# A fused attention and Fourier-mixing kernel on one core: the first batch's softmax sums leave TensorE, and the weights' rounding is spread into the second batch

## The chip, the cores and the metric

One core of a Trainium2 chip runs the whole kernel. The engines are named as in the profile: PE (TensorE matmuls), PEld (its weight loads), DVE (VectorE), ACT (ScalarE), POOL (GpSimd), SP (SyncE, which issues most DMAs). The metric is the device time of one execution in microseconds (us); less is better.

## The reference, cut to what matters

Four batches of eight heads over 768 positions with 64 columns each. Block-sparse attention, then a Fourier mixing block with a feed-forward part over 512 columns:

```python
scores = scale * np.matmul(q, k.transpose(0, 1, 3, 2))
scores = np.where(mask, scores, -1000000000.0)
scores = scores - np.max(scores, axis=-1, keepdims=True)
attn = np.exp(scores)
attn = attn / (np.sum(attn, axis=-1, keepdims=True) + 1e-09)
x = ...  # matmul(attn, v), heads side by side: (4, 768, 512)
mixed = np.real(np.fft.fft(np.fft.fft(x, axis=1), axis=2))
u = x + mixed
un = (u - mean(u)) / np.sqrt(var(u) + 1e-06)
out = u + np.maximum(un @ w_ch1, 0.0) @ w_ch2   # 512 x 2048, 2048 x 512
```

The mask is made from 32 x 32 blocks, some of them drawn at random. The two weights arrive in float64.

## The kernel before

**Attention in slots.** Heads are taken in 16 pairs, four to a batch. A pair has 12 units (two halves of the queries, six chunks of 128 keys), and a *slot* is two units, so a pair has six slots, a batch 24, the whole attention 96. `slot(sl)` writes the instructions of one slot: `scores` (the products `s`, L573, and for the first batches the mask as a second product, L583), `weigh` (the exponential on ScalarE, L593, into one of four `e` buffers), and, for the slot before, `values` (products `o` with v, L647). At the end of a pair the results are turned and copied into `x` (`place`). For pairs 5 and on, q and k are transposed by VectorE (`flip_blocks`, L540) and q put in order by ScalarE (`in_order`, L548).

**The softmax sums.** The sum over keys of every query is needed to divide by. Batch 0 gets it on TensorE: `add_up` multiplies each `e` by a column of ones into the PSUM tile `sp` (L714), and `into_sums` adds it to `sums`. In batches 1 to 3 `gather` adds the six chunks of a half into `acc`, either in one addition on VectorE (L628) or in two of half the width on GpSimd (L633), whichever the planner thinks sooner (the last two units of a pair always on GpSimd); `total` then needs only one set of products a pair (L728). An `e` buffer is free when both its values and its addition are done.

**The mixing.** When a batch's attention is complete, `begin(b)` queues its mixing in `apart`, a list in fixed order: `norm_steps` (`invert` turns the sums and takes reciprocals, `scale_x` multiplies, L756), eight folds on VectorE (`fold_0`, ...; L779 to L807), four products along the sequence (`along`, `zp`), three across (`across`, `pq`), then for each of six tiles `arrive`, `spread` (statistics), `whiten`, `un_flip` (transposes `utp`, copies) and the sums `left` and `right` for a Strassen product. At its end `go()` moves the channel steps into `late`: eight `quad` (seven products each, L1045) and 24 `channels` (L1101); it also ends the masking by products. While batch b mixes, batch b+1's attention goes on.

**The planner.** The order on each engine is written by the program itself (`manual_schedule`), by a ledger `when` of planned times: `busy(engine, us)` adds a price, and `gap` takes the next step of `apart` only if the ledger says that its inputs are ready and that VectorE isn't more than a few us ahead (`AHEAD`, `ALONE`). `until(met)` takes steps whether or not they are ready, until a condition holds. One of these is hard: `x` has two buffers, so in slot 53 the first result of batch 2 has to wait `until(lambda: (b - 2, 0) in finished)`, that is until all channel steps of batch 0's first half are written.

**The weights.** They come as 32 chunks of 128 x 512, which a DMA brings raw (float64) into one of five rooms (`W_ROOMS` 0, 1, 3, 4, 5 of the pool `big`; the mixing uses the same rooms later), and `w_round` rounds to float32: two ScalarE operations (L460, L463) and five on VectorE (L464 to L472), priced 1.2 and 3.0. `w_loads` and `w_steps` stand at the end of each slot; with `W_PACE = 1.42` chunks a slot, all 32 are rounded by slot 22, all of `w_ch1` first.

Of the kernel before, what the change touches and what calls it, by code (L numbers as in the profile page):

```python
# [102 lines left out]
def kernel(  # L103
# [332 lines left out]
    WN = 512  # L436
    wchunks = []
    for w, w_sb in ((w_ch1, w1_sb), (w_ch2, w2_sb)):
        rows, cols = w.shape
        words = _words(w, rows * cols)  # L440
        for row in range(rows // P):
            for col in range(0, cols, WN):
                src = bass.AP(tensor=words, offset=2 * (row * P * cols + col),
                              ap=[[2 * cols, P], [1, 2 * WN]])
                wchunks.append((src, w_sb[:, row, col:col + WN]))
    wraw = {}
    W_ROOMS = (0, 1, 3, 4, 5)

    def w_load(i):
        t = room(W_ROOMS[i % len(W_ROOMS)], [P, 3 * WN], "wraw", U32)  # L450
        nc.sync.dma_start(out=t[:, 0:2 * WN].bitcast(I32), in_=wchunks[i][0])
        wraw[i] = t

    def w_round(i):
        t = wraw.pop(i)
        dst = wchunks[i][1]
        pair = t[:, 0:2 * WN].rearrange("p (n two) -> p n two", two=2)
        lo, hi, a = pair[:, :, 0], pair[:, :, 1], t[:, 2 * WN:3 * WN]

        nc.scalar.mul(out=lo.bitcast(FP32), in_=lo, mul=2.0 ** -52)  # L460


        nc.scalar.mul(out=a.bitcast(FP32), in_=hi.bitcast(FP32), mul=2.0 ** -112)  # L463
        nc.vector.tensor_scalar(out=a, in0=a, scalar1=3, scalar2=0x7FFFFFFF,  # L464
                                op0=ALU.logical_shift_left, op1=ALU.bitwise_and)
        nc.vector.scalar_tensor_tensor(out=dst.bitcast(U32), in0=hi, scalar=0x80000000, in1=a,
                                       op0=ALU.bitwise_and, op1=ALU.bitwise_or)

        nc.vector.tensor_scalar(out=a, in0=dst.bitcast(U32), scalar1=0xFF800000, scalar2=None,
                                op0=ALU.bitwise_and)  # L470
        nc.vector.tensor_mul(out=a.bitcast(FP32), in0=lo.bitcast(FP32), in1=a.bitcast(FP32))
        nc.vector.tensor_add(out=dst, in0=dst, in1=a.bitcast(FP32))  # L472
        busy("DVE", 3.0, busy("ACT", 1.2))
# [11 lines left out]
    turned, e_of, acc_of, o_of, sums_of, x_of, sp_of = {}, {}, {}, {}, {}, {}, {}  # L485
# [101 lines left out]
    def weigh(u, s):  # L587
        n, w = divmod(u, UP)
        half, c = divmod(w, C)
        e = ep.tile([P, 2, HS], FP32, tag="e", name="e")  # L590
        e_of[u] = e
        if u in by_pe:
            nc.scalar.activation(out=e, in_=s[:, :, 0:HS], func=ACT.Exp, scale=scale)  # L593
            e_at[u] = busy("ACT", 0.8, max(s_at[u], e_free.pop(u - 2 * SLOT, 0.0))) + HOP
            if n >= NP:
                to_gather.append(u)

            if w >= UP - SLOT:
                gather_to(u)
        else:  # L600
            nc.scalar.activation(out=s[:, :, 0:HS], in_=s[:, :, 0:HS], func=ACT.Exp, scale=scale)  # L601
            m = mask[:, c, half * HS:(half + 1) * HS].rearrange("p (o s) -> p o s", o=1)
            nc.vector.tensor_tensor(out=e, in0=s[:, :, 0:HS], in1=m.broadcast_to([P, 2, HS]),  # L603
                                    op=ALU.mult)
            e_at[u] = busy("DVE", 0.97, busy("ACT", 0.8, s_at[u]) + HOP) + HOP
            gather_to(u)
            if n >= NP:
                gather(u)
# [5 lines left out]
    def gather(u):  # L614
# [11 lines left out]
        sooner = max(when["DVE"], at) + 1.0 < max(when["POOL"], at) + 2.9  # L626
# [3 lines left out]
        else:  # L630
# [3 lines left out]
            acc_at[n, half] = busy("POOL", 2.9, at) + HOP  # L634
# [55 lines left out]
    def into_sums(key, j, sp):  # L690
        if j == 0:
            if key == (0, 1):
                sums_of[key] = un_p.tile([P, DM], FP32, tag="un", name="sums")[:, 0:HS]
            else:
                sums_of[key] = sum_p.tile([P, HS], FP32, tag="sums", name="sums")
# [3 lines left out]

    def add_up(us):  # L700


        n, w = divmod(us[0], UP)
        half, c = divmod(w, C)
        j = pairs[n][1]
        if c == 0:
            sp_of[n, half] = ps_m.tile([P, 512], FP32, tag="m", name="sp"), bank("m")
        sp, at = sp_of[n, half]
        sp = sp[:, 0:HS]
        busy("PE", 0.85)  # L710
        for r, u in enumerate(us):
            for i in range(2):
                g = BLK * (2 * i + r)
                nc.tensor.matmul(sp[g:g + BLK, :], pick[:, BLK - j:2 * BLK - j], e_of[u][:, i, :],  # L714
                                 start=(c == 0), stop=(c == C - SLOT), tile_position=(0, g))
        if c == C - SLOT:
            into_sums((0, half), j, sp)
            give(at, busy("DVE", 0.6, when["PE"] + HOP))
# [14 lines left out]
    def norm_steps(b):  # L733
# [3 lines left out]
        def invert(half):  # L737
            sums = sums_of.pop((0, half) if b == 0 else b)
# [4 lines left out]
            if b > 0:  # L743
                nc.vector.reciprocal(out=r, in_=st[:, :, :, 0:NP])
                return
            for i in range(2):
                to = r[:, :, 2 * half + i, :]
                nc.vector.tensor_copy(out=to, in_=st[:, :, 2 * i, 0:NP])
                nc.vector.tensor_tensor(out=to, in0=st[:, :, 2 * i + 1, 0:NP], in1=to, op=ALU.add)
            if half == 1:  # L750
                nc.vector.reciprocal(out=r, in_=r)
# [7 lines left out]
        return ([("t", lambda h=h: invert(h), 0.45, 0.0, 0.9) for h in range(2 if b == 0 else 1)] +  # L759
# [8 lines left out]
    def fourier(b, xA, xB, uns):  # L768
# [6 lines left out]
        def fold_0(i):  # L775
            if i == 0:
                st["f"] = (room(0, [P, T, DM], "sa"), room(1, [P, T, DM], "sd"),
                           un_p.tile([P, DM], FP32, tag="un", name="e1"))
# [114 lines left out]
        def arrive(half, m):  # L893
# [13 lines left out]
            tt(out=ends, in0=un[:, 0:M + 1:M], in1=ends, op=ALU.add)  # L907

# [47 lines left out]
    def mixer(b, xA, xB):  # L956
# [27 lines left out]
        def spare_room():  # L984
            if s:
                return
            rest, n, w = room(5, [P, ND * HS], "t4"), HS * ND // 2, P * ND // 2
# [25 lines left out]
        def left(p, j):  # L1013
# [3 lines left out]
            spare_room()  # L1017
            a11, a12, s2, a22 = blocks(p)
# [78 lines left out]
        def channels(r, half, m):  # L1097

            y, at = ps_m.tile([P, DM], FP32, tag="m", name="y"), bank("m")
# [150 lines left out]
    W_PACE = 1.42  # L1250
# [3 lines left out]
    state = {"paired": False, "total": None, "w": 0, "got": 0, "owed": 0.0, "ready": 0.0}  # L1254
# [91 lines left out]
    def w_loads():  # L1346
        while state["got"] < min(len(wchunks), state["w"] + len(W_ROOMS)):
            w_load(state["got"])
            state["got"] += 1

    def w_steps(sl):
        while state["w"] < min(len(wchunks), W_PACE * sl):
            w_round(state["w"])
            state["w"] += 1

    def slot(sl):
# [7 lines left out]
        def sum_up():  # L1364
# [5 lines left out]
            if at < SB:  # L1370
                add_up(done)
# [57 lines left out]
        if sl > SB and s == 0 and sl <= B * SB:  # L1429
# [66 lines left out]
    w_load(0)  # L1496
    load_q(1)
    w_load(1)
    load_k(1)
    state["got"] = 2  # L1500
# [118 lines left out]
```

## Time and profile before

| what | us |
|---|---|
| median of 3 runs | 1062.0 (1061.76 to 1062.73) |
| span of the profiled execution | 1059.7 |
| PE busy | 1036.7 |
| DVE busy | 654.7 |
| ACT busy | 374.3 |
| POOL busy | 235.6 |
| `add_up` products (L714) | 20.5 busy |
| `total` products (L728) | 10.9 busy |

The profiled execution is a run of its own; the page gives its span, from the first instruction to the last, and that span is what the trace's durations are added up against. It is 2.3 us shorter than the median of the timed runs. A matmul in float32 shows as two instructions (x192 for 96 products). In a timeline the columns are start, length, engine, line, operation, output and inputs, count, and in brackets the idle time before and what ended it. In a table of groups the numbers behind the bar are busy us, mean ns of one, and the idle time before them.

### The profile page before, as it was taken

Reading aid. Unit: us, or ns where it says so; the run is one execution under the profiler, and the core shown is the slowest. Engines: PE = TensorE matmul, PEld = TensorE weight load, DVE = VectorE, ACT = ScalarE, POOL = GpSimd, SP = SyncE. Lnnn points to the kernel's source line nnn. Section 1 sums busy time; section 2 is a strip of 40 time slices with the busy share of each in tenths; the row PEclk is TensorE's granted clock in tenths of the full one; section 3 lists DMA queues with packets and bytes.
Section 4 is the critical chain, followed back from the end, with each engine's and each line's share of the span. In section 5 each row is a group of like instructions: output and inputs, shape, how many; then the busy total and the mean of one; then the engine's idle time right before and its main releaser. Section 6 shows DMA issues by size and latency. Waiting matters only on the chain.

```text
span 1059.7 us, 12422 instructions
## 1 busy us (share of the span) xinstructions
PE 1036.7 (98%) x4390; PEld 535.8 (51%) x4390; DVE 654.7 (62%) x1218; ACT 374.3 (35%) x742; POOL 235.6 (22%) x262
## 2 busy tenths in 40 slices
PE   8999999999999999999999999999999999999996
PEld 4333345444455554444444555444445554578575
DVE  6898894667645445664668364765457455575663
ACT  6978855664030112342441302253220211210210
POOL 1000183537000002454553001256520001000000
PEclk9999999999999999999999999999999999999998
DMA  7757422220000002212220001221000001000001
GB/s 214 231 168 232 117 46 45 45 47 15 1 0 1 1 0 48 59 29 54 42 54 2 1 0 30 60 38 28 11 11 6 1 0 32 29 0 1 1 20 43
DMA packets 120803, 46.65 MB, mean 44 GB/s; under 512 B 108176, under 2 KB 113822, under 8 KB 120734
## 3 DMA queue, kind: packets, MB, share of 16 engines
q1 hardware_dynamic: 119484, 45.06, 17.3%
q10 hardware_dynamic: 1218, 0.72, 0.3%
q8 instruction: 36, 0.59, 0.2%
q14 instruction: 33, 0.27, 0.1%
q0 software_dynamic: 32, 0.01, 0.0%
HBM read 37.11 MB, written 6.29 MB: 41 GB/s over the span
## 4 chain that ended last, share of the span: by engine, by line
PE 89%; DVE 4%; DMA 3%; ACT 2%; issue 1%; SPq 0%; POOL 0%; ACTq 0%; DVEq 0%
PE y L1101 23%; PE z L1045 15%; PE s L573 12%; PE o L647 10%; PE yp L1045 7%; PE yy L1164 7%; PE xp L1045 4%; PE zp L855 2%; DMA out_dram<-x 1%; PE s L583 1%; PE zp L827 1%; PE sp L714 1%; PE sp L728 1%; PE utp L970 1%; PE xt L670 1%
## 5 line engine op out<-in xcount | busy, mean ns | idle before, releaser
L633 POOL TENSOR_TENSOR acc<-acc,e 128x384 f32<-128x384 f32 x158 | 159.3, 1042 | 94.1 <-DVE e L603 75.1
L573 PE MATMUL s<-qT,kT 64*128 64x384 f32 x768 | 154.0, 516 | 7.7 <-ACT e L593 4.3
L647 PE MATMUL o<-e,vr 128*64 128x384 f32 x768 | 141.8, 497 | 0.0
L1101 PE MATMUL y<-w_sb,hB 128*128 128x512 f32 x288 | 128.2, 596 | 1.0 <-DVE x L1104 1.0
L1101 PE MATMUL y<-w_sb,hA 128*128 128x512 f32 x288 | 128.4, 595 | 0.0
L603 DVE TENSOR_TENSOR e<-s,mask 128x768 f32<-128x768 f32 x92 | 83.8, 951 | 57.6 <-ACT s L601 47.8
L1104 DVE TENSOR_TENSOR x<-y,x 128x512 f32<-128x512 f32 x72 | 49.7, 690 | 110.9 <-PE y L1101 110.8
L573 PEld LDWEIGHTS s<-qT,kT 64*128 64x128 f32 x768 | 64.2, 186 | 85.8 <-issue 22.1
L601 ACT ACTIVATE s<-s 128x768 f32<-128x768 f32 x92 | 69.9, 792 | 87.5 <-PE s L573 87.0
L1045 PE MATMUL z<-unT,t 128*128 128x384 f32 x256 | 93.1, 486 | 1.2 <-DVE hA L1050 1.2
L633 POOL TENSOR_TENSOR acc<-e 128x384 f32<-128x384 f32 x42 | 47.1, 1142 | 211.6 <-ACT e L593 126.7
L1050 DVE TENSOR_TENSOR hA<-z,hA 128x384 f32<-128x384 f32 x64 | 35.7, 557 | 87.5 <-PE z L1045 87.5
L593 ACT ACTIVATE e<-s 128x768 f32<-128x768 f32 x100 | 76.1, 815 | 36.2 <-PE s L583 31.2
L1101 PEld LDWEIGHTS y<-w_sb,hB 128*128 128x128 f32 x288 | 53.4, 190 | 67.7 <-issue 65.0
L918 POOL TENSOR_SCALAR st<-st 128x1 f32<-128x1 f32 x24 | 8.6, 358 | 346.9 <-DVE st L917 346.8
L1101 PEld LDWEIGHTS y<-w_sb,hA 128*128 128x128 f32 x288 | 53.3, 190 | 62.8 <-issue 59.7
L647 PEld LDWEIGHTS o<-e,vr 128*64 128x64 f32 x768 | 47.9, 136 | 70.3 <-issue 67.9
L1054 ACT ACTIVATE hA<-hA 128x384 f32<-128x384 f32 x64 | 33.5, 523 | 120.3 <-DVE hA L1050 119.9
L1045 PEld LDWEIGHTS z<-unT,t 128*128 128x128 f32 x256 | 48.5, 190 | 35.5 <-DVE hA L1050 2.1
L1054 ACT ACTIVATE hB<-hB 128x384 f32<-128x384 f32 x64 | 33.5, 523 | 86.5 <-DVE hB L1050 84.2
L1065 ACT COPY hA<-xp 128x384 f32<-128x384 f32 x32 | 15.3, 478 | 97.9 <-PE xp L1045 97.9
L1045 PE MATMUL xp<-unT,w_sb 128*128 128x384 f32 x128 | 47.2, 492 | 0.0
(202 smaller groups left out, 1428.7 us busy)
## 6 DMA issues: line engine op xcount, KB each, us to landing
wraw<-in_moe_w_ch_dram SPq DMA_DIRECT2D x32, 512.0 KB
vr<-in_v_dram SPq DMA_DIRECT2D x30, 192.0 KB
qb<-in_q_dram SPq DMA_DIRECT2D x44, 96.0 KB
kb<-in_k_dram SPq DMA_DIRECT2D x44, 96.0 KB
x<-oT SPq DMA_DIRECT2D x192, 12.0 KB
out_dram<-x SPq DMA_DIRECT2D x15, 128.0 KB
out_dram<-x SPq DMA_DIRECT2D x7, 256.0 KB
qr<-in_q_dram SPq DMA_DIRECT2D x24, 64.0 KB
```

Source lines behind the costliest of these rows:

```text
L573: nc.tensor.matmul(s[:, i, 0:HS], kT[rows, c * P:(c + 1) * P], qT[rows, queries], start=True, stop=u not in by_pe)
L593: nc.scalar.activation(out=e, in_=s[:, :, 0:HS], func=ACT.Exp, scale=scale)
L601: nc.scalar.activation(out=s[:, :, 0:HS], in_=s[:, :, 0:HS], func=ACT.Exp, scale=scale)
L603: nc.vector.tensor_tensor(out=e, in0=s[:, :, 0:HS], in1=m.broadcast_to([P, 2, HS]), op=ALU.mult)
L633: nc.gpsimd.tensor_add(out=acc[:, i, :], in0=start[:, i, :], in1=e[:, i, :])
L647: nc.tensor.matmul(o[D * i:D * i + D, :], vt[:, i, c, :], e[:, i, :], start=(c == 0), stop=(c == C - 1))
L1045: nc.tensor.matmul(to, a[:, k, :], c[:, k, :], start=(k == 0), stop=(k == ND // 2 - 1))
L1050: tt(out=to, in0=ps, in1=a, op=ALU.add)
L1054: nc.scalar.activation(out=h, in_=h, func=ACT.Relu)
L1101: nc.tensor.matmul(y, hs[0, half][:, l, m * P:(m + 1) * P], w2_sb[:, 4 * r + l, :], start=(l == 0), stop=(l == 3))
L1104: nc.vector.tensor_tensor(out=x[:, m, :], in0=y, in1=x[:, m, :], op=ALU.add)
L1164: nc.tensor.matmul(ps, a[:, k, :], c[k // 2][:, k % 2, :] if isinstance(c, list) else c[:, k, :], start=(k == 0), stop=(k == 3))
```

## The change

Four things, in one diff. (1) Batch 0's sums go the way of the other batches: `add_up` and the second `invert` are gone, `gather` runs for all batches, `total` for all pairs. (2) The chunks are listed in the order in which the channel steps need them: four of `w_ch1`, four of `w_ch2`, and so on. (3) `W_PACE` is 0.6: `w_until(int(0.6 * sl))` at the end of each slot, so that 14 chunks are rounded by slot 24 and the last ones in slots 52 to 54; `w_until` in `left`, `spare_room` and `channels` rounds at once what a step needs. (4) A raw chunk takes any room that is free; `w_leave` gives rooms back to the mixing, rounding first what lies in them: 0 and 1 at `fold_0` (returned after the last `arrive` of batch 0), 3, 4 and 5 at `spare_room`. The planner's prices for a rounding (3.0 to 3.6 on VectorE) and for an addition on GpSimd (2.9 to 2.2) change too.

```diff
+    for r in range(NF // 4):
+        wchunks += [wchunk(w_ch1, w1_sb, row, r * WN) for row in range(ND)]
+        wchunks += [wchunk(w_ch2, w2_sb, 4 * r + l, 0) for l in range(4)]
+    wraw, w_room = {}, {}
+    w_state = {"got": 0, "done": 0, "rooms": (0, 1, 3, 4, 5)}
+
+    def w_load():
+        i = w_state["got"]
+        if i == len(wchunks):
+            return False
+        free_of = [r for r in w_state["rooms"] if r not in w_room.values()]
+        if not free_of:
+            return False
+        w_room[i] = free_of[0]
+        t = room(w_room[i], [P, 3 * WN], "wraw", U32)
         nc.sync.dma_start(out=t[:, 0:2 * WN].bitcast(I32), in_=wchunks[i][0])
         wraw[i] = t
+        w_state["got"] += 1
+        return True
+
+    def w_until(n):
+        while w_state["done"] < min(n, len(wchunks)):
+            if w_state["done"] == w_state["got"]:
+                w_load()
+            w_round(w_state["done"])
+            del w_room[w_state["done"]]
+            w_state["done"] += 1
+
+    def w_leave(*rooms, to=None):
+        if w_state["done"] < len(wchunks):
+            w_state["rooms"] = tuple(r for r in w_state["rooms"] if r not in rooms)
+            w_until(max([i + 1 for i, r in w_room.items() if r in rooms], default=0))
+            w_state["rooms"] += tuple(to or ())
...
-        busy("DVE", 3.0, busy("ACT", 1.2))
+        busy("DVE", 3.6, busy("ACT", 1.2))
...
-            if n >= NP:
-                to_gather.append(u)
+            to_gather.append(u)
...
-        sooner = max(when["DVE"], at) + 1.0 < max(when["POOL"], at) + 2.9
+        sooner = max(when["DVE"], at) + 1.0 < max(when["POOL"], at) + 2.2
...
-    def add_up(us):
...
         def fold_0(i):
             if i == 0:
+                w_leave(0, 1)
...
+            if m == 1 and half == 1 and b == 0:
+                w_leave(to=(0, 1))
...
         def spare_room():
             if s:
                 return
+            w_leave(3, 4, 5)
+            w_until(8)
...
+            w_until(8 * (p // 2) + 4)
...
+            w_until(8 * r + 8)
...
-    W_PACE = 1.42
+    W_PACE = 0.6
...
     def w_steps(sl):
-        while state["w"] < min(len(wchunks), W_PACE * sl):
-            w_round(state["w"])
-            state["w"] += 1
+        w_until(int(W_PACE * sl))
...
-            if at < SB:
-                add_up(done)
...
-        if sl > SB and s == 0 and sl <= B * SB:
+        if 0 < sl <= B * SB and s == 0:
             short.append(("t", acc_at[n - 1, 1], lambda: total(n - 1)))
```

## The prediction

> **What bounds the kernel now.** I read the shares by slice first, then the chain that ended last, then stages. The chain is TensorE's almost everywhere:
>
> ```profile
> PE   8999999999999999999999999999999999999996
> DVE  6898894667645445664668364765457455575663
> POOL 1000183537000002454553001256520001000000
> ...
> PE 89%; DVE 4%; DMA 3%; ACT 2%; issue 1%; SPq 0%; POOL 0%; ACTq 0%; DVEq 0%
> ```
>
> So a microsecond taken from TensorE's queue is worth a microsecond, as long as no other engine becomes late. The two stages that the change touches are the first batch (slots 2 to 23, 15.84 to 123.33 us) and the second up to its first channel product (123.33 to 241.80). The stage table (length, then busy time of PE, PEld, DVE, ACT, POOL):
>
> ```profile
> 15.84:123.33 107.49, 103.36 (x694) 41.58 (x693) 95.21 (x204) 93.11 (x193) 0.00 (x0) 0.98 0.67 201
> 123.33:241.80 118.47, 117.50 (x717) 54.10 (x717) 82.92 (x134) 73.85 (x146) 61.10 (x58) 1.00 0.25 48
> 161.00:178.00 17.00, 17.00 (x87) 8.93 (x85) 6.37 (x6) 9.27 (x21) 5.92 (x6) 1.00 0.19 31
> ```
>
> In both TensorE is the bound, but VectorE has only 12 us to spare in the first and 35.6 in the second, of which 10.6 lie in 161 to 178, where the mixing waits for TensorE's `zp` products. GpSimd is idle in the first.
>
> **First batch, TensorE.** The groups by form, the one long stall in TensorE's timeline, and its cause among the waits (us in total, times, longest):
>
> ```profile
> L714 PE MATMUL sp<-e,pick 128*32 128x384 f32 x192 | 20.5, 498 | 0.0
> L728 PE MATMUL sp<-acc,pick 128*32 128x384 f32 x96 | 10.9, 497 | 0.1
> ...
> 66.76 0.85 PE L714 MATMUL sp<-e,pick 128*32 128x384 f32 x8
> 70.01 2.46 PE L573 MATMUL s<-qT,kT 64*128 64x384 f32 x8 [2.40 <-ACT e L593]
> ...
> 76.11 1.56 PE L573 MATMUL s<-qT,kT 64*128 64x384 f32 x8
> ...
> ACT wraw L460 <- DMA wraw<-in_moe_w_ch_dram: 3.8, 2, 3.3
> ```
>
> `add_up` runs once in each of 24 slots. Start to next start it takes 0.78 us (14.25 to 15.03): 24 x 0.78 = 18.7 us removed. `total`, 0.79 us (182.00 to 182.79), is added for four pairs, three of them inside the stage: +2.4, the fourth +0.8 after it; one of two sums transposes (133.94 to 134.42) goes, -0.5. At 67.6 ScalarE waits 3.3 us for a raw chunk and TensorE stands for 2.40; then the matmuls up to the next scores take 6.2 us (70.01 to 76.19) for work that takes 4.6 elsewhere. Rounding 0.6 chunks a slot instead of 1.42 asks for about 19 chunks in this stage (14 rounded, 5 raw) instead of 32, so I take these 2.4 + 1.6 = 4.0 us as gone too.
>
> A slot then needs 4.89 - 0.78 - 0.18 + 0.11 = 4.04 us of TensorE (4.89 is 107.49 / 22). Can the others keep that pace? VectorE: a chunk takes 2.97 us (18.75 to 21.73), so 1.8 a slot, and tables and sums 0.4. The sums are ten additions a pair, 1.67 a slot, at 1.04 us on VectorE (L628) or about 2.2 on GpSimd (two of 1.04 to 1.14, L633). One on GpSimd and 0.67 on VectorE gives GpSimd 2.2 and VectorE 2.9 of 4.04. ScalarE loses 18 chunks x 1.14 us. So they fit, but the two disturb each other:
>
> ```profile
> 124.78 0.69 DVE L472 TENSOR_TENSOR w_sb<-w_sb,wraw 128x512 f32<-128x512 f32 x1
> ...
> 126.56 0.43 DVE L469 TENSOR_SCALAR wraw<-w_sb 128x512 uint32<-128x512 uint32 x1
> 127.03 1.37 DVE L471 TENSOR_TENSOR wraw<-wraw 128x512 f32<-128x512 f32 x1
> 128.43 1.37 DVE L472 TENSOR_TENSOR w_sb<-w_sb,wraw 128x512 f32<-128x512 f32 x1
> ...
> 126.75 2.50 POOL L633 TENSOR_TENSOR acc<-e 128x384 f32<-128x384 f32 x2 [121.65 <-ACT e L593]
> ```
>
> The moment GpSimd adds, the two-tensor operations of the rounding double: a chunk beside GpSimd takes 2.97 + 2 x 0.68 = 4.33 us. With GpSimd busy for half a slot that is 0.4 us more a slot on VectorE, 3.3 in all: still inside 4.04. For late additions that hold an `e` buffer I put 2.5 us (between 0 and 8). The second batch therefore starts 18.7 - 2.4 + 4.0 - 2.5 = 17.8 us earlier; with the fourth total and the transpose, 17.5.
>
> **Second batch: what the rounding meets there.** Until now it was free of rounding but for a tail of 6.1 us (the L464 to L472 rows up to 129.73). By the pace, 14 chunks are done by slot 24 and 31 by slot 52, whatever else waits: 17 chunks, 17 x 2.97 = 50.5 us on VectorE alone, 73.6 beside GpSimd. VectorE's sum: 82.9 - 6.1 + 50.5 = 127.3 us if its own additions (20.5 us, L628) stay. If they all go to GpSimd, that has 61.1 + 20 x 2.2 = 105 of 118 us, is beside the rounding nearly always, and VectorE has 76.8 - 20.5 + 73.6 = 129.9. Either way some 128 us, against this much of TensorE before the channel products must start:
>
> ```profile
> 241.82 1.46 PE L1045 MATMUL xp<-unT,w_sb 128*128 128x384 f32 x4
> ...
> 256.74 1.72 PE L573 MATMUL s<-qT,kT 64*128 64x384 f32 x8
> 258.39 1.56 PE L1045 MATMUL xp<-unT,w_sb 128*128 128x384 f32 x4
> ...
> 409.07 1.56 PE L573 MATMUL s<-qT,kT 64*128 64x384 f32 x8
> ```
>
> The last scores before a long stretch of products stand at 256.74: slot 53, after which the third batch needs the tiles that batch 0 holds, and the program lets no attention through until batch 0 is finished. The mixing now reaches its first product at 241.82 with 6.0 us of attention left (252.37 to 258.39). So TensorE has 118.5 + 6.0 = 124.5 us of other work for the second batch's VectorE chain to hide under, and 1.7 more when the mask products of slots 50 to 53 (0.42 each) come back, since `go()` comes later.
>
> Add to 128 the idle time that the chain's own dependences force: 35.6 today; rounding fills part of it; 10 to 15 stay, the 161 to 178 kind. That is 138 to 143 us, TensorE idle for 12 to 17 at the wall. The second way to the same number goes by order. The rounding at each slot's end isn't asked whether there is room, while a mixing step is placed only if VectorE's planned lead stays under 3 to 4.5 us. At the planner's price of 3.6 us each and 3 chunks in 5 slots, mixing gets only the rest; walking down the slots by those prices, I have `fold_0` in slot 34 instead of 28, with three chunks at once in front of it (`w_leave(0, 1)`), and at slot 53 everything from the second `spread` on still to do. At the trace's durations these steps are: five `spread` 3.9, five `whiten` 2.3, one `across` 0.8, two `arrive` 1.7, `left` with one chunk 4.1, `right` 4.3: 17 us of VectorE, and 7 of product, transpose, copy and GpSimd waits between them, with 5.5 us of TensorE in it: 18.5 idle. I take 19 (between 4 and 28), since there nothing covers it. Two queues stand behind a backlog on VectorE: ScalarE's `in_order` copies wait for VectorE's transpose of q and hold the exponentials behind them; SP's weight loads wait for a room and hold the q, k, v loads. Both have a slot or more of slack, so I cost them at nothing; without it, each is a slot's 3 to 4 us.
>
> After the gap the matmuls start slow, as at 70.01: +1.6. The Trainium skill ("TensorE: Matmul & The Clock Gate", Part 1) has the clock fall only after an idle window of about 3.4 us; 2.40 us sufficed in the rows above, so the rows decide, and by the page this term would be nought.
>
> **Sum** against the profiled execution, 1059.7 us: -17.5 + 19 + 1.6 + 1.7 = +4.8, 1064.5. The median of the runs shown is 1062.0, 2.3 above the span: 1066.8, say 1066. What follows the wall has no part in the change: one chunk is left, under products. Under 0.2% (2.1 us) a measurement of this kernel can't tell from no change.
>
> **The rivals.**
> - *The second batch absorbs the rounding* (faster). The chain is ahead of my ledger because rounding falls into the 161 to 178 kind of hole and the real chunk is 2.97, not 3.6. It decides the sign where the idle time at the wall is under 14 us. With 6 us left: 1062 - 17.5 + 6 + 1.7 = 1052; with none 1046. For it: VectorE's idle 35.6 us; against: 128 of 124.5. Chance 0.33.
> - *GpSimd and VectorE bind the first batch too* (slower still). If all five operations of a chunk double beside GpSimd, a chunk is 5.9 us, 3.6 a slot, and with 1.1 of other work VectorE passes 4.04: the slot grows to 4.6, 12 us of the 17.5 are lost, and the wall is no earlier: 1062 - 5.5 + 22.3 = 1079. The L469 row (0.43 with GpSimd beside it for its second half) speaks against. The Trainium skill ("GPSIMD Engine Reference", Key points) speaks for it: contention with every VectorE instruction that has two SBUF inputs or a two-port mode. Chance 0.12.
> - *The pace is not what sets the rounding*: rooms that leave force the chunks at two points, and in between nothing is rounded, the chain runs free and the wall idles some 14: about 1062, no change. Chance 0.08.
>
> **How the numbers follow.** The forecast has 0.47, its own range 1058 to 1073 (idle 11 to 26). Its low edge lends 0.04 to faster and 0.03 to same. Faster: 0.33 + 0.04 = 0.37. Same: 0.08 + 0.03 = 0.11. Slower: 0.40 + 0.12 = 0.52. The range of 8 in 10 leaves out half of the second rival and the best end of the first: 1048 to 1077.
>
> **What would show it.** Right: no L714; slot 24 some 18 us earlier; scores of slot 23 about 4.1 us apart; VectorE over 95% busy from there to the wall; `fold_0` five or more slots later; before the first `xp` a stretch of 15 to 25 us in which TensorE does transposes and stands. Wrong: the first `xp` still two slots before the last scores, or first-batch slots over 4.5 us.

## The result, and the profile after

The kernel after takes 1100.95 us (1099.45 to 1101.06), the kernel before on the same chip 1062.03: a ratio of 1.0364 (1.0349 to 1.0378). Forecast were 1066 us and a range of 1048 to 1077, so the sign was right and the size was not. The profiled execution spans 1099.3 us, 39.6 more than before. The page of after, its slices and its chain:

```profile
PE   8998966988699999999999999999999999999996
DVE  5887988899874544565567646575456455575663
POOL 4877874766400000154547000155450001000000
PEclk9999986999799999999999999999999999999999
...
PE 78%; DVE 13%; issue 3%; ACT 2%; DMA 2%; SPq 1%; POOL 0%; DVEq 0%; ACTq 0%
```

Nearly all that changed lies in the first 11 slices. There GpSimd is busy for 4 to 8 tenths of every slice, TensorE shows a 6 in slices 6, 7 and 11, the clock falls to 6 and 7 tenths in the last two of these, and VectorE's share of the chain goes from 4% to 13%. The stages, in the columns of the stage table of before (length; busy PE, PEld, DVE, ACT, POOL; clock). The first two rows are slots 2 to 23 and slot 24 to the first channel product; that second stretch is called *the stage* from here on. The third row is its worst stretch, the fourth is from slot 53 to that product:

```profile
15.02:113.01 97.99, 91.64 (x543) 39.55 (x542) 78.22 (x112) 72.66 (x155) 74.25 (x64) 0.98 0.50 141
113.01:288.45 175.44, 136.44 (x767) 60.91 (x767) 156.92 (x190) 98.76 (x188) 121.86 (x106) 0.89 0.32 79
...
165.12:184.34 19.22, 8.25 (x43) 3.24 (x40) 18.81 (x19) 4.07 (x8) 12.82 (x10) 0.70 0.32 75
...
269.09:288.45 19.36, 8.61 (x46) 4.88 (x45) 17.74 (x23) 7.12 (x12) 16.74 (x18) 0.75 0.00 1
```

Slot 24 starts at 113.01 instead of 123.33: 10.3 us gained, not 17.8. From there to the first product it takes 175.44 us, where the prediction counted 124.5 us of TensorE's work: 51 lost (the prediction had 146.8 us for it, 22.3 lost). The difference of the two, 40.6, is the 39.6 of the span to within 1 us. TensorE stands still for 175.44 - 136.44 = 39.0 us of it; the rest is mostly matmuls at the low clock. What it waited for from slot 24 to that product (us in total, times, longest):

```profile
PE s L599 <- DVE kT L566: 19.6, 3, 11.0
PE s L599 <- ACT e L619: 8.1, 7, 3.3
PE utp L967 <- DVE un L927: 7.4, 3, 7.0
```

The longest of these waits, in the timeline: VectorE rounds four chunks one after the other, with GpSimd adding beside it until 178.22; then come `fold_0` (`sa`) and, behind all of it, the transpose of k for which ScalarE's squares of k and TensorE's scores wait.

```profile
167.78 10.44 POOL L658 TENSOR_TENSOR acc<-acc,e 128x384 f32<-128x384 f32 x8
...
170.81 1.21 DVE L490 TENSOR_SCALAR wraw<-wraw 128x512 uint32<-128x512 uint32 x1
...
172.06 1.37 DVE L492 SCALAR_TENSOR_TENSOR w_sb<-wraw 128x512 uint32<-128x512 uint32 x1
173.47 1.10 DVE L495 TENSOR_SCALAR wraw<-w_sb 128x512 uint32<-128x512 uint32 x1
174.60 1.36 DVE L497 TENSOR_TENSOR wraw<-wraw 128x512 f32<-128x512 f32 x1
176.00 1.37 DVE L498 TENSOR_TENSOR w_sb<-w_sb,wraw 128x512 f32<-128x512 f32 x1
...
181.06 1.75 DVE L774 TENSOR_TENSOR sa<-x 128x1536 f32<-128x1536 f32 x1
182.72 1.47 DVE L566 STREAM_TRANSPOSE kT<-kb 128x768 f32<-128x768 f32 x1
...
184.34 2.93 PE L599 MATMUL s<-qT,kT 64*128 64x384 f32 x8 [10.97 <-DVE kT L566]
```

Two things are to be read here. All five operations of a chunk are long beside GpSimd, not two: start to next start the chunk takes 170.81 to 177.29, 6.48 us, against 2.97 before. And the scores behind the wait take 2.93 us instead of 1.56.

### The profile page after: what moved, and what is told of

Read it like the earlier page. It is cut to its first block, busy times and chain, and to the rows that moved or that the text cites. A ratio compares the mean times of both kernels' runs of the same rounds, so it can differ in the third digit from the quotient of the medians.

```text
span 1099.3 us, 12224 instructions
## 1 busy us (share of the span) xinstructions
PE 1038.0 (94%) x4243; PEld 538.5 (49%) x4243; DVE 711.1 (65%) x1189; ACT 375.8 (34%) x742; POOL 356.2 (32%) x360
## 4 chain that ended last, share of the span: by engine, by line
PE 78%; DVE 13%; issue 3%; ACT 2%; DMA 2%; SPq 1%; POOL 0%; DVEq 0%; ACTq 0%
PE y L1102 22%; PE z L1045 15%; PE s L599 9%; PE yp L1045 7%; PE o L672 7%; PE yy L1165 6%; PE xp L1045 4%; DVE wraw L497 2%; DVE w_sb L492 2%; DVE wraw L495 2%; PE zp L850 1%; DVE wraw L490 1%; PE zp L822 1%; DVE t L1006 1%; PE utp L967 1%
## 5 line engine op out<-in xcount | busy, mean ns | idle before, releaser
L658 POOL TENSOR_TENSOR acc<-acc,e 128x384 f32<-128x384 f32 x238 | 262.6, 1135 | 101.0 <-DVE e L628 64.5
L599 PE MATMUL s<-qT,kT 64*128 64x384 f32 x768 | 158.8, 529 | 29.0 <-DVE kT L566 19.6
L672 PE MATMUL o<-e,vr 128*64 128x384 f32 x768 | 144.9, 505 | 0.0
L628 DVE TENSOR_TENSOR e<-s,mask 128x768 f32<-128x768 f32 x84 | 76.5, 951 | 49.0 <-ACT s L626 39.1
L658 POOL TENSOR_TENSOR acc<-e 128x384 f32<-128x384 f32 x60 | 68.0, 1152 | 116.9 <-PE sp L730 106.5
L619 ACT ACTIVATE e<-s 128x768 f32<-128x768 f32 x108 | 82.4, 809 | 59.6 <-PE s L609 38.8
L626 ACT ACTIVATE s<-s 128x768 f32<-128x768 f32 x84 | 63.7, 792 | 84.7 <-PE s L599 84.6
```

The lines of the kernel that those rows point to most:

```text
L599: nc.tensor.matmul(s[:, i, 0:HS], kT[rows, c * P:(c + 1) * P], qT[rows, queries], start=True, stop=u not in by_pe)
L658: nc.gpsimd.tensor_add(out=acc[:, i, :], in0=start[:, i, :], in1=e[:, i, :])
L672: nc.tensor.matmul(o[D * i:D * i + D, :], vt[:, i, c, :], e[:, i, :], start=(c == 0), stop=(c == C - 1))
```

## The experiments

Three theories stood at first. **P**: VectorE and GpSimd stretch each other wherever the one rounds while the other adds. **V**: there is simply too much work on VectorE. **B**: the four chunks in one go ahead of `fold_0` make the loss. Each kernel ran once, beside the kernel before on the same chip (1061.1 to 1061.7 us).

### The two parts alone

The sums alone, with the old pace (the chunks' order and rooms and the planner's prices stay as in the kernel after):

```diff
-    W_PACE = 0.6
+    W_PACE = 1.42
```

> The changed kernel with the old pace of rounding, 1.42 chunks a slot: all 32 chunks are rounded in the first batch, beside GpSimd's new additions. Theory P (the port: VectorE's operations with two SBUF inputs or in a two-port mode double while GpSimd adds, so that a chunk costs up to 6.5 us instead of 3.0): 32 chunks at about 5 us are 160 us, the first batch grows from 107 to 150 us or more, total 1095 to 1115 us. Theory V (VectorE simply has too much in the second batch, whatever GpSimd does): the first batch has its 12 us of room, gains some 10 us, the second is as before: 1050 to 1060 us. Theory B (only the burst at fold_0 hurts): as V.

Measured: 1115.05 us. Slot 24 starts at 159.32 instead of 123.33, and 144 us on, at 303.21, comes the first channel product. With the rounding beside GpSimd the first batch alone loses 36 us, where V and B had it gaining; so GpSimd is no free place for the sums. The time is at the upper end of P's range; the first batch grew to 144 us, where P had 150 or more. The weights alone, with `add_up` on TensorE as before (the prices stay here too):

```diff
-            to_gather.append(u)
+            if n >= NP:
+                to_gather.append(u)
...
+            if at < SB:
+                add_up(done)
```

> The changed kernel with the first batch's sums on TensorE again (add_up, two inverts). GpSimd is idle in the first batch, in the second all is as in the change. All three theories put the loss of the second batch (51 us) here too; the first batch keeps its 107 us less up to 4 for the DMA wait: 1100 to 1110 us. If it comes out under 1085, the first batch's sums do harm beyond the first batch. P alone says that a chunk costs 3.0 us up to slot 24 and 5 and more after it.

Measured: 1107.6 us. Slot 24 starts at 117.83, 5.5 us early (the stall for raw chunks is gone), and the first product stands at 295.94, 178 us later. The second batch's loss is whole without the first batch's sums: it belongs to the rounding that was moved there. A chunk's five operations on VectorE take 2.93 us in the mean up to slot 24, where GpSimd is idle, and 4.94 after it, as P alone had it.

### Less of the one, less of the other

GpSimd's additions of pairs 4 to 8 made 8 columns wide (c > 1), so that most of those softmax sums are left out:

```diff
+            cols = slice(0, 8 if 4 <= n <= 8 and c > 1 else HS)
             for i in range(2):
-                nc.gpsimd.tensor_add(out=acc[:, i, :], in0=start[:, i, :], in1=e[:, i, :])
+                nc.gpsimd.tensor_add(out=acc[:, i, cols], in0=start[:, i, cols],
+                                     in1=e[:, i, cols])
```

> The changed kernel, but in pairs 4 to 8 (second batch and a little after) four of five GpSimd additions of a half are 8 columns wide instead of 384: most of those softmax sums are left out, the order of all instructions is unchanged. P: a chunk falls from 5.05 us to about 3.3 in the second batch, VectorE has 30 us less, the waits for kT fall from 19.6 us to under 5, total 1055 to 1070 us. V: a chunk may change but the queue stays late by its volume: 1090 to 1100. B: the burst of four chunks stays in front of kT, at half its length: 1080 to 1090.

Measured: 1067.92 us, as P had it. The stage, in the columns of the stage table:

```profile
111.69:255.97 144.28, 130.88 (x768) 60.18 (x767) 116.70 (x190) 97.43 (x188) 53.98 (x106) 0.95 0.40 97
```

So of the 51 us lost 31 go with the width of GpSimd's additions alone, and 19.8 are left. Next, the other side made narrow: from chunk 14 on four of the five VectorE operations of a rounding work on 8 columns, which leaves out most of the rounding of 18 chunks, with GpSimd as it is.

> The changed kernel, but from chunk 14 on four of the five VectorE operations of a rounding are 8 columns wide: most of the rounding of 18 chunks is left out, the order is unchanged. P, V and B all say that the second batch then takes about what it did before, 125 to 135 us instead of 175; with the 10 us gained in the first batch 1050 to 1062 us. If more than 1075 remains, the loss isn't VectorE's rounding but the order that the planner's prices made.

Measured: 1074.36 us, which no theory had. The timeline of VectorE says why: with GpSimd adding (first chunk shown) an operation on 8 columns takes 0.92 us, and 0.17 where GpSimd stands (second).

```profile
126.44 0.92 DVE L500 TENSOR_TENSOR wraw<-wraw 128x8 f32<-128x8 f32 x1
127.39 0.92 DVE L501 TENSOR_TENSOR w_sb<-w_sb,wraw 128x8 f32<-128x8 f32 x1
...
144.86 0.17 DVE L500 TENSOR_TENSOR wraw<-wraw 128x8 f32<-128x8 f32 x1
145.06 0.17 DVE L501 TENSOR_TENSOR w_sb<-w_sb,wraw 128x8 f32<-128x8 f32 x1
```

So the price is not paid by the column. An operation is held by some 0.7 us, whatever its own length: 0.17 to 0.92, 0.43 to 1.10, 0.69 to 1.37. Both narrow at once:

> The kernel after with both edits at once: the GpSimd additions of pairs 4 to 8 and, from chunk 14 on, four of the five VectorE operations of the rounding are 8 columns wide; most of those sums and roundings are left out. It asks what the 19.8 us are that stay lost between slot 24 and the first product of the channels when only GpSimd is made narrow. Theory V for this remainder (VectorE's volume, as the prediction had it): they go nearly all, 1046 to 1054, first product within 130 us of slot 24. Theory O (the order that the planner wrote, with late mixing steps and a chain that nothing covers, whatever the operations cost): most of them stay, 1060 to 1068, 138 to 145 us.

Measured: 1056.94 us, between the two theories. The stage:

```profile
111.76:245.97 134.21, 126.19 (x768) 57.50 (x768) 88.52 (x190) 96.62 (x188) 46.63 (x106) 0.99 0.42 104
```

That divides the 51 us: 31.2 for GpSimd's width, 10.1 more for that of the rounding (144.28 to 134.21), and 9.7 that stay with neither: 1.7 of mask products (126.19 - 124.5, the prediction's term) and 8.0 of standing.

### GpSimd's additions with nobody waiting for them

Are the long operations caused by the other engine, or by waits between the two? In the kernel *before*, GpSimd idles in the first batch. There it was given additions on a tile of its own:

```diff
+        if 4 <= sl < 16:
+            d = state["idle"]
+            for i in range(2 if sl < 10 else 8):
+                cols = slice(0, HS if sl < 10 else 96)
+                nc.gpsimd.tensor_add(out=d[:, 0, cols], in0=d[:, 0, cols], in1=d[:, 1, cols])
```

> The kernel before, with GpSimd additions in the first batch that nothing waits for: in slots 4 to 9 two of 128 x 384 a slot, in slots 10 to 15 eight of 128 x 96, none after. It measures by itself what an addition on GpSimd does to a rounding on VectorE. Theory P (a VectorE operation stands still for the length of the GpSimd instruction beside it, whatever its kind and width): a chunk takes 4 to 6 us start to end in slots 4 to 9, 3.5 to 5 in slots 10 to 15, 2.97 after; 1064 to 1075, since VectorE had 12 us to spare. If only the operations on two tensors are disturbed: 3.5 to 4.4 us in slots 4 to 9 and the 0.43 us rows (L464, L469) stay. If the stretch seen in the second batch came from waits and not from the port: 2.97 throughout, 1061 to 1062.

Measured: 1073.64 us, 12.0 slower by work that nothing needs. Two chunks in the timeline, the first beside additions of 384 columns, the second beside those of 96; then the two groups of GpSimd (busy, mean ns):

```profile
41.50 1.23 DVE L464 TENSOR_SCALAR wraw<-wraw 128x512 uint32<-128x512 uint32 x1
...
42.77 1.37 DVE L466 SCALAR_TENSOR_TENSOR w_sb<-wraw 128x512 uint32<-128x512 uint32 x1
44.17 1.11 DVE L469 TENSOR_SCALAR wraw<-w_sb 128x512 uint32<-128x512 uint32 x1
...
62.38 0.76 DVE L466 SCALAR_TENSOR_TENSOR w_sb<-wraw 128x512 uint32<-128x512 uint32 x1
63.17 0.50 DVE L469 TENSOR_SCALAR wraw<-w_sb 128x512 uint32<-128x512 uint32 x1
```

```profile
L1359 POOL TENSOR_TENSOR idle<-idle 128x96 f32<-128x96 f32 x48 | 27.7, 578 | 3.8
L1359 POOL TENSOR_TENSOR idle<-idle 128x384 f32<-128x384 f32 x12 | 14.6, 1218 | 31.8 <-DVE idle L1354 30.9
```

The first chunk takes 6.52 us (41.50 to 48.02), one beside the narrow additions 3.27 (61.91 to 65.18), one alone 2.97. After the first addition no wait ties the two engines here, so the stretch is the pairing itself. "4 to 6 us" was too little for the wide additions, and "3.5 to 5 us" too much for the narrow ones: the hold depends on GpSimd's *instruction* (0.7 us beside one of 384 columns, 0.07 beside one of 96). GpSimd pays for the narrow ones: four of 96 take 2.3 us, one of 384 1.22.

### Is it an order, or VectorE's whole time?

The burst ahead of `fold_0` taken out, by keeping rooms 0 and 1 free of raw chunks from slot 20 on:

```diff
     def w_steps(sl):
+        if sl == 20:
+            w_state["rooms"] = (3, 4, 5)
```

> The kernel after, but rooms 0 and 1 take no raw chunk from slot 20 on, so that fold_0 finds them free and the four chunks rounded in one go ahead of it (165 to 181 us in the kernel after) are spread by the pace instead. Nothing is left out. Theory B (the burst ahead of fold_0 makes the loss): the 10.97 us wait of the scores for kT and the slow matmuls behind it go, 15 to 20 us, so 1080 to 1086. Theory P (VectorE and GpSimd stretch each other, wherever the rounding stands): the wait moves and shrinks but the stretch stays, 1092 to 1098. Theory V (too much volume on VectorE): no change, 1099 to 1102.

Measured: 1099.01 us. The 11.0 us wait is gone (kT 9.3 in all instead of 19.6), but `utp` now waits 16.1 us for `un` instead of 7.4. B is refuted. The time is V's, a little above P's range. The same again with the queue itself: attention's transposes sooner.

```diff
-            for at, fn, args in ((0, squares, (n + 1, 0)), (1, flip_blocks, (n + 1, 0)),
-                                 (2, in_order, (n + 1,)), (4, flip_blocks, (n + 1, 1)),
+            for at, fn, args in ((0, squares, (n + 1, 0)), (0, flip_blocks, (n + 1, 0)),
+                                 (2, in_order, (n + 1,)), (2, flip_blocks, (n + 1, 1)),
```

> The kernel after, but VectorE's transposes of the next pair's q and k are issued one and two slots sooner (slots 0 and 2 of a pair instead of 1 and 4), ahead of the roundings that they stood behind; nothing is left out. Theory Q (the loss is the queue: attention's transposes behind rounding): the 19.6 us wait of the scores for kT and most of the slow matmuls behind it go, 1070 to 1082, and the first channel product comes 20 us sooner. Theory T (VectorE's whole time up to the first channel product is overcommitted, and a wait that is taken away in one place comes up in another): the kT wait goes below 6 us, the waits of utp for un grow by as much, 1094 to 1102.

Measured: 1099.25 us. TensorE's waits from slot 24 on, and the stage:

```profile
PE utp L967 <- DVE un L927: 9.1, 3, 8.6
PE xt L695 <- DVE sums L718: 8.6, 1, 8.6
PE s L599 <- ACT e L619: 6.1, 5, 1.9
```

```profile
111.91:286.79 174.88, 137.85 (x768) 61.31 (x767) 160.35 (x189) 98.99 (x188) 127.58 (x108) 0.90 0.33 80
```

Not one wait for kT is left, and the stage is 174.88 us instead of 175.44: the waits went to VectorE's other work. VectorE is busy for 92% of it. In these two kernels, then, a change of the order at one place decides who waits and not how long the stage is. Then the additions back to VectorE, where its chunks would be short again:

```diff
-        if u in by_pe and masks["by_pe"] and w < UP - SLOT and sooner:
+        if u in by_pe and masks["by_pe"] and w < UP - SLOT:
```

> The kernel after, but gather takes VectorE for every unit where its rule lets it (the last two units of a pair stay on GpSimd), in the first and the second batch alike; nothing is left out. VectorE gets some 1.04 us for each addition that GpSimd loses, in all about 25 additions more in the second batch's stretch. Theory V (volume on VectorE): 15 to 25 us slower than after, 1115 to 1125. Theory P (contention): a chunk falls from 5.05 towards 2.97 us on VectorE, 19 chunks x 2 = 38 us less against 25 us more, and the first batch likewise, so faster than after: 1080 to 1095, with fewer L490 to L498 rows above 1 us. If P holds with the whole price, the first product of the channels comes within 165 us of slot 24.

Measured: 1103.65 us; neither. VectorE's groups in the stage (busy, mean ns), and the stage itself:

```profile
L653 DVE TENSOR_TENSOR acc<-acc,e 128x768 f32<-128x768 f32 x32 | 30.5, 953 | 1.1
L492 DVE SCALAR_TENSOR_TENSOR w_sb<-wraw 128x512 uint32<-128x512 uint32 x19 | 15.2, 800 | 0.6
L497 DVE TENSOR_TENSOR wraw<-wraw 128x512 f32<-128x512 f32 x20 | 14.5, 727 | 0.7
...
113.95:292.50 178.55, 134.30 (x768) 59.73 (x767) 146.83 (x227) 100.10 (x190) 31.60 (x36) 0.91 0.32 78
```

The five operations of a chunk come to 3.26 us (5.05 in after): some 34 us less. But VectorE now makes 42 additions instead of 5: 37 x 0.95 = 35 us more. Counted on the roundings alone, an addition costs VectorE as much when GpSimd makes it beside a rounding as when VectorE makes it itself: P and V were two prices of one thing.

That does not explain the time, though. Other operations became shorter too, and in all VectorE is busy for 146.83 us, 10.1 less than in after (156.92); yet the stage is 3.1 us longer. The order changed with the edit: `fold_0` stands in slot 45 (216.23 us) instead of 35, and from slot 53 to the first product there are 43.1 us instead of 19.4. The planner books these additions on VectorE, and `gap` keeps mixing steps back while VectorE is ahead by the ledger; that this is what moved `fold_0` is argued and was not tried. So this run prices an addition and does not decide between P and V.

### How much rounding the second batch bears

These kernels are the one before, or the weights' part alone (order of need, sums on TensorE), with one number changed: the pace.

> The kernel before with W_PACE 1.37 instead of 1.42: the last chunk in slot 23. If the 4 us stall for raw chunks hangs on the rate, some 2 to 4 us go, 1057 to 1060; if the second batch's order is upset by every change of its start as with 1.32, 1063 to 1067; no change at all, 1061 to 1062.5.

> The kernel before with one number changed, W_PACE 1.32 instead of 1.42, so that the last chunk is rounded in slot 24 instead of 22. If the 2.40 us wait of ScalarE and TensorE for a raw chunk at 67.6 us comes from the rate at which chunks are asked for, it goes with the slow matmuls behind it: 4 us less, 1057 to 1060. If the stall has to do with where the loads stand in the queue and not with their rate, it stays: 1061 to 1063.

> The kernel before with W_PACE 1.22 instead of 1.42: the last chunk in slot 26. With 1.32 slot 24 came 4.3 us earlier and the second batch lost 8 us, in one 4.1 us wait behind GpSimd's additions of 1.9 us each beside the folds. If that loss is an accident of the order, 1056 to 1061 here; if rounding in slots 24 to 26 costs by itself, 1063 to 1068.

> The weights' part of the change alone (sums of the first batch on TensorE, chunks in order of need, any free room), but at 1.25 chunks a slot instead of 0.6, so that nearly all rounding is over before the second batch's GpSimd additions begin in earnest. Theory P and V agree: the loss in the second batch goes with the rounding, and the 4 to 5.5 us of the missing stall for raw chunks stay as a gain, 1055 to 1060. If the second batch's order suffers from any shift of its start, 1063 to 1070.

Measured, in this order: 1061.25, 1065.33, 1070.42 and 1069.83 us. The first is no change; the second and third lie above everything that was expected; the fourth is in the range of an order that suffers from any shift.

| kernel | chunks ended between slot 24 and the first product | slot 24 starts | against before | lost from slot 24 on |
|---|---|---|---|---|
| before, pace 1.42 | 2 | 123.33 | 0 | 0 |
| pace 1.37 | 3 | 122.80 | -0.4 | 0.1 |
| pace 1.32 | 4 | 119.05 | +3.7 | 8.0 |
| pace 1.22 | 6 | 118.20 | +8.8 | 13.9 |
| order of need, 1.25 | 6 | 117.61 | +8.2 | 13.9 |
| order of need, 0.6 | 20 | 117.83 | +46.2 | 51.7 |
| after | 19 | 113.01 | +38.9 | 49.2 |

The last column is the fourth plus what slot 24 came sooner (in us). From the third row on it is 2.9 to 4 us for every chunk past the second. The count of chunks is not all of it: the sums alone ended four there and lost 17.6 us from slot 24 on, with 9.4 in one wait for `sums`. At 1.22 the largest part can be seen in one chain of the timeline, in order of time:

```profile
130.87 1.37 DVE L466 SCALAR_TENSOR_TENSOR w_sb<-wraw 128x512 uint32<-128x512 uint32 x1
...
136.10 0.96 DVE L540 STREAM_TRANSPOSE qb<-qb 128x768 f32<-128x768 f32 x1
...
137.15 1.88 ACT L548 COPY qT<-qb 128x256 f32<-128x256 f32 x6 [7.21 <-DVE qb L540]
...
140.90 1.65 PE L573 MATMUL s<-qT,kT 64*128 64x384 f32 x4 [7.38 <-ACT e L593]
```

Two stretched chunks stand ahead of the transpose of q, ScalarE's copies wait 7.21 us for that with the exponentials behind them, and the scores wait 7.38 for those. That wait is 7.4 of the 13.9 us, and the scores behind it are slow.

Can the missing stall be kept as a gain? At 1.32 slot 24 comes 4.3 us sooner, and a wait of 4.1 us for ScalarE's copy of `x` takes it back: it stands behind exponentials that wait for GpSimd additions of 1.93 us each (7.71 for four) beside the folds. Four tries at it: a pace of 1.32 with all rounding that is left written at the end of slot 23; the same with fewer additions on GpSimd; and either with the order at that wait as it was before.

```diff
-        while state["w"] < min(len(wchunks), W_PACE * sl):
+        while state["w"] < min(len(wchunks), (1.32 if sl < 23 else W_PACE) * sl):
...
-        sooner = max(when["DVE"], at) + 1.0 < max(when["POOL"], at) + 2.9
+        sooner = max(when["DVE"], at) + 1.0 < max(when["POOL"], at) + 4.0
...
-            at = oT_at[n - 1, 1]
+            at = oT_at[n - 1, 1] + (2.0 if b == 1 else 0.0)
```

> The kernel before with 1.32 chunks a slot up to slot 22 and the rest in slot 23, so that the raw chunks are asked for more slowly and yet all are rounded when the second batch begins. Since 1.32 alone took away the stall and lost 8 us in the second batch, and 1.37 left both as they were: 1056 to 1060 if the second batch goes as with 1.37, 1063 to 1067 if as with 1.32.

> As d1, and the planner's price of an addition on GpSimd is 4.0 instead of 2.9, so that gather takes VectorE more often in batches 1 to 3. If GpSimd's additions cost VectorE more than the planner knows, 1054 to 1059; if VectorE is short of time in these batches, 1062 to 1070.

> As d1, and the planner's due time for turning the last results of the second batch's first pair is 2.0 us later, so that the sums' products (L728) stand before those transposes again, as in the kernel before. In d1 they stood behind them and waited 4.1 us for ScalarE's copy, which stood behind exponentials that waited for GpSimd additions of 1.93 us each beside the folds. If that order is what gave the missing stall's gain back: 1057 to 1060. If the second batch loses it elsewhere whatever the order: 1063 to 1067.

> As d2 (price of a GpSimd addition 4.0 in the choice) with the later due time of d7. If both help: 1055 to 1058. If the order alone matters, the same as d7 within 1 us; if the second batch loses it elsewhere: 1062 to 1066.

Measured: 1065.69, 1063.85, 1064.83 and 1064.96 us, against 1061.1 to 1061.7 before. The first two still have the 4.1 us wait; with the third and fourth it is gone, and the time is the same. So the order at that wait isn't the reason. But in all four kernels four chunks still ended after slot 24 began, as at 1.32, and from slot 24 on they lose 7.2 to 8.1 us, as 1.32 does (8.0). What they were built to try, the smoother pace with all rounding done by slot 24, they did not reach, and by which waits these 7 to 8 us are lost stays open. Of the kernels that leave nothing out none is faster than before by more than 0.4 us.

## Why the prediction was wrong

**The sign and the order of the chain were right.** `add_up` (L714) is gone, and the stall for raw chunks too: the weights alone bring slot 24 forward by 5.5 us, priced 4.0. `fold_0` stands where the walk through the planner's prices had it, with four chunks ahead of it where three were counted (165.12 to 181.06, slots 34 and 35). The mask products of four slots came back, as counted. Of the other signs that were named, slot 24 came 10.3 us earlier and not 18, and VectorE was busy for 89% of the stage and not over 95%.

**The step that failed is the price of a chunk beside GpSimd**: "2.97 + 2 x 0.68 = 4.33 us". It was read from the rows from 126.56 to 129.80, of which two were doubled and one, L469 at 126.56, was not; but GpSimd began at 126.75, after that row had started, and a row that started before GpSimd's tells nothing of what happens to its operation. Measured are 5.05 us in the mean of the second batch, 5.2 in the first and 6.48 where GpSimd never pauses, all five operations long. VectorE's groups in the stage of the kernel after (busy, mean ns):

```profile
L497 DVE TENSOR_TENSOR wraw<-wraw 128x512 f32<-128x512 f32 x19 | 21.3, 1120 | 0.7
L498 DVE TENSOR_TENSOR w_sb<-w_sb,wraw 128x512 f32<-128x512 f32 x19 | 21.2, 1118 | 0.6
L492 DVE SCALAR_TENSOR_TENSOR w_sb<-wraw 128x512 uint32<-128x512 uint32 x19 | 20.6, 1086 | 0.7
L495 DVE TENSOR_SCALAR wraw<-w_sb 128x512 uint32<-128x512 uint32 x19 | 17.7, 932 | 0.7
L490 DVE TENSOR_SCALAR wraw<-wraw 128x512 uint32<-128x512 uint32 x19 | 15.1, 794 | 7.1 <-ACT wraw L489 7.1
```

The 19 chunks come to 95.9 us against the 73.6 that 17 were priced at, in a stage where VectorE had been found 128 us of work for 124.5 us of cover. VectorE was already the bound in the forecast, so an error of its price had nothing to hide under: it was busy for 156.9 us instead of 129.9, 27.0 us more, and the stage took 175.4 instead of 146.8, 28.6 more. That the first goes over into the second nearly whole holds for the order that this kernel has; with the additions on VectorE it did not. In the first batch there was room for the same error, since VectorE was busy there for 78 of 98 us.

The rival that had this price ("all five operations", 0.12) was therefore right in the price and wrong in the place. It came to 1079 because it put the new price into the first batch, which had room for it, and left the second at the old one. The Trainium skill speaks to it on a page that the prediction did not use: "SBUF — State Buffer", section "Who interferes with whom", says that a VectorE instruction with two SBUF inputs contends with a GpSimd instruction that reads SBUF. It says the same of VectorE in a two-port mode, and that whichever engine issues first has the shared port pair for the whole instruction while the other is blocked. The runs agree in what they show: the hold is 0.7 us beside an addition of 384 columns, 0.07 beside one of 96, and does not depend on VectorE's own width; VectorE's transposes (L566 of qb, 0.97 us here and 0.96 before) are not held.

**A second consequence was missing: the clock.** 1.6 us was priced for one slow start. TensorE was busy for 136.44 us in a stage whose work takes 126.19 with both sides narrow, at a clock of 0.99: 10.2 us more, behind 39.0 us of waits. On average a wait cost its own length and about a quarter more. The remark that the term "would be nought" with an idle window of 3.4 us did not follow from the forecast either, which had 18.5 us of idle time in one stretch; the longest single wait there was 7.0 us.

**Where TensorE stands was not forecast.** The prediction put all 19 us of it at the wall. Measured are 10.7 us there (19.36 - 8.61) and 28.2 us ahead of it, from slot 24 to slot 52, where it had put nothing. The stretch from slot 53 to the first product has the length that was named, but 19.4 us of it with 8.6 of TensorE's work at a clock of 0.75 are not the 24 us with 5.5 that were priced: that the two agree is luck. It is luck too that the stage came to 144.3 us, near the 146.8 of the forecast, with GpSimd's additions narrow: VectorE was busy for 116.7 us there and not for the 129.9 of the forecast.

**The two queues "costed at nothing"** were the right ones to name: the waits for kT are 19.6 us, and at a pace of 1.22 the chain through `in_order` is the largest part of the loss. But they are not a term that can be added to the others: with the queue taken away (transposes early) the time stayed, since VectorE then made others wait.

**The first batch** gave 10.3 us for 17.8. The failed terms are `total`, 2.4 us for three, and the 2.5 for late additions. The three products that fall into the stage took 1.42, 1.95 and 5.40 us, start to next start. The last two units of a pair are always GpSimd's, so `total` stands at the head of TensorE's queue until GpSimd is through:

```profile
85.97 0.84 PE L730 MATMUL sp<-acc,pick 128*32 128x384 f32 x4
...
89.03 0.83 PE L730 MATMUL sp<-acc,pick 128*32 128x384 f32 x2 [2.22 <-POOL acc L658]
...
90.43 1.01 PE L730 MATMUL sp<-acc,pick 128*32 128x384 f32 x2 [0.57 <-POOL acc L658]
91.37 2.93 PE L599 MATMUL s<-qT,kT 64*128 64x384 f32 x8
```

With 1.3 us for the slow scores behind it that is 10.1 us, where 4.9 were priced (2.4 + 2.5): 5.2 of the 7.5 missing. The rest is of the size of TensorE's other waits in slots 2 to 23 (3.1 us, for ScalarE's copies and the sums on VectorE); that it is these was not tried. The split of the additions was wrong as well: one a slot on GpSimd was assumed; 64 halves, that is 32 additions, in 22 slots are 1.45.

## What to carry to other kernels

Work that is moved from a full engine to GpSimd is not off VectorE's hands. In this case every operation of the rounding was held by about 0.7 us beside GpSimd's additions of 384 columns, so what the two engines do side by side has to be added up as one resource before anything is counted as hidden. Read the price of such a pairing from rows where both engines run throughout, and measure it, if it isn't in the trace, with idle instructions that nothing waits for. Where an engine is overcommitted, a wait that is taken out in one place can come up in another: compare its whole busy time with the cover before its queues. That sum is a first look and not the time: here a kernel with 10 us less on VectorE was slower, with its mixing steps placed later.

## What the runs showed of the hardware that was not expected

- A VectorE operation of 8 columns took 0.92 us beside GpSimd's additions of 384 columns and 0.17 without; beside additions of 96 columns one of 512 columns took 0.76 instead of 0.69. GpSimd's own additions of 384 columns went from 0.97 us (four in 3.86 at 192.41 in the kernel before, with VectorE idle for most of it) to 1.32 beside roundings (eight in 10.56 at 137.12 in the kernel after).
- After a wait of 2.2 us and one of 0.57 the scores took 2.93 us instead of 1.56; after one of 11 us the same 2.93. In the stage with 39.0 us of waits the granted clock was 0.89.
